# Two half feed-forward units for batches 0 to 3 in place of one full unit

## Chip, cores and metric

The kernel runs on one NeuronCore of a Trainium2 chip. The metric is the device time of one execution in microseconds, of which the median of several runs is taken. The engines are named as in the profile: PE (matrix multiply; PEld is its weight load), DVE (vector), ACT (scalar), POOL (GpSimd) and SP, whose queue issues most transfers.

## What is computed

Top-k attention for 8 batches, 8 heads, 576 tokens and head size 64, followed by a feed-forward block on its 4608 x 512 output:

```python
scores = scale * np.matmul(q, k.transpose(0, 1, 3, 2))
kth = np.partition(scores, -top_k, axis=-1)[..., -top_k:-top_k + 1]
mask = scores >= kth
...
attn = np.exp(scores)
attn = attn / (np.sum(attn, axis=-1, keepdims=True) + 1e-09)
return np.matmul(attn, v).astype(np.float32)
...
h = x @ w_in
g = h - np.tanh(h)
return (g @ w_out).astype(np.float32)
```

Here top_k is 32, w_in is 512 x 2048 and w_out is 2048 x 512. All data are float32.

## The kernel before

**Steps.** The attention is cut into 144 steps, 18 a batch. A main step handles 128 queries of one pair of heads. Since 576 is 4 x 128 + 64, the last 64 tokens of a batch are left over; two remainder steps a batch handle them, each for two pairs of heads. A step's scores are made by PE (L351), copied by ACT (L359) and searched by DVE (L381 to L404) for the 32nd largest value. L381 is the first instruction of a step on DVE. The bank of the scores is read by DVE until L389, and the next step's scores go into the same bank. Then ACT and POOL mask (L437, L440), ACT takes the exponential (L460) and divides (L486), and DVE turns the result in blocks of 32 (L518) into the buffer zx. SP writes zx to DRAM (L531) and reads it back in another order (L534), and five steps later PE multiplies by the values (L582). In batch 0 the turning goes by PE instead. The rows of q and k of batches 1 and 2 are transposed by PE (L311), those of the others by DVE (L318).

**Units.** The attention output, transposed (xT for main tokens, xTr for the leftover ones), goes to the feed-forward block in units. A unit of two blocks has 256 tokens; one of a single block has 128. The leftover 64 tokens of four batches make one unit of 256: batches 0 to 3 and batches 4 to 7. xTr has one buffer.

**Work items.** When a unit's last values are there, `ffn` appends its work to a queue, as items that issue 8 matmuls each (16 records in the profile, since each float32 matmul is recorded twice).
- A full unit has 16 items of `ffn_h` (x @ w_in, tanh, difference): each matmul is split by `by_columns` in two halves of 64 columns of weights with 256 moving columns (L626). Every second item ends with tanh (L652), a copy (L653) on ACT and a difference on POOL (L654). Then come 14 items of `ffn_p`: seven products instead of eight, by a scheme of sums and differences of the quarters. It has the sums made on POOL (L828), its partial results copied by ACT (L909 to L926) and joined on POOL (L877), and two of its right sides, T4 and T2, brought from DRAM by SP (L834).
- A single-block unit has 8 items of `ffn_h` with the full 128 columns of weights and 128 moving columns (L640), and 8 items of `ffn_small_o` (L661). Before the change these are two units of batch 0 only.

When the first full units run, POOL overwrites the upper right corner of each w_out piece by its difference to the upper left one (`combine`, T1), so the products use T1 in place of that corner.

**Order.** Nothing schedules the program afterwards: `run` writes the order by hand. In each step `rate` sets how many items are to be dealt: the smallest rate at which the queue would be empty just when one of the coming units is ready, and at least the one at which a unit's buffer is free in time. `deal` then issues 0.4 of them ahead of the next step's scores, and the rest in three parts of 0.2 behind them. Each engine runs in this order; items that stand ahead of scores on PE come first.

```python
for t, k in coming + [(NS + LAG, 0)]:
    r = have / max(t - n, 1)
    high = r if high is None else min(high, r)
    have += k
...
def deal(part):
    nonlocal credit
    credit += part * share
    while work and credit > 0 and work[0][0] <= usable:
        work.pop(0)[2]()
        credit -= 1
    credit = min(credit, 1.0)
```

Behind the last step a tail remains, in which the last two units run with almost only PE busy. A second pass with an exact search stands behind a branch that is taken only when the fast search failed.

Of the kernel before, what the change touches and what calls it, by code (L numbers as in the profile page):

```python
# [9 lines left out]
ALU = mybir.AluOpType  # L10
FP32 = mybir.dt.float32
# [8 lines left out]
J = 4  # L20
# [35 lines left out]
def kernel(  # L56
# [9 lines left out]
    nc = tc.nc  # L66
    P = nc.NUM_PARTITIONS
    B, H, S, D = q.shape
    DM, DFF = moe_w_in.shape
    NHP = H // 2  # L70
    JP = J * P
    R = S - JP
# [4 lines left out]
    CD = DM // P  # L77
# [5 lines left out]
    WJ = 4  # L83
    FJ = CF // WJ
# [6 lines left out]
    def pool(name, bufs, **kw):  # L91
        return ctx.enter_context(tc.tile_pool(name=name, bufs=bufs, **kw))
# [10 lines left out]
    thpool = pool("th", 4)  # L103
# [7 lines left out]
    bank = [0]  # L111

    def h_bank(k, name):
        return h_ps.tile([P, 512], FP32, tag=f"h{k}", name=name)

    def next_h(name):
        bank[0] ^= 1
        return h_bank(bank[0], name)
# [6 lines left out]
    w_out = [consts.tile([P, FJ, DM], FP32, name=f"w_out{j}") for j in range(WJ)]  # L125
# [91 lines left out]
    def half(t):  # L217
        return slice(t * D, (t + 1) * D)
# [118 lines left out]
    rest = consts.tile([P, 2, S4 + Q], FP32, name="rest")  # L337
# [230 lines left out]
    def values(n):  # L568
# [41 lines left out]
        if n in done:  # L610
            work.extend(ffn(u))
# [9 lines left out]
    cur = {}  # L621

    def by_columns(acc, lhs, rhs, start, stop):

        for t in range(2):
            nc.tensor.matmul(  # L626
                acc[half(t)], lhs[:, half(t)], rhs, start=start, stop=stop, skip_group_check=True
            )
# [45 lines left out]

    def corners(x):
        x = x.rearrange("p (m r) n -> p m r n", r=2)
        return [[x[:, :, r, c * 2 * P : (c + 1) * 2 * P] for c in range(2)] for r in range(2)]

    def keep_corner(j):

        nc.sync.dma_start(kept_B12[:, 2 * j : 2 * j + 2, :], corners(w_out[j][:])[0][1])

    def bring_corners():

        for j in range(WJ):
            nc.sync.dma_start(corners(w_out[j][:])[0][1], kept_B12[:, 2 * j : 2 * j + 2, :])

    def combine(x, j):  # L690

        (b11, b12), (b21, b22) = corners(w_out[j][:])
        k, ms = j // 2, slice(2 * (j % 2), 2 * (j % 2) + 2)
        t2 = whole["T2"][k][:, ms, :]
        if x == "T3":
            nc.gpsimd.tensor_tensor(whole["T3"][k][:, ms, :], b12, b22, ALU.subtract)
        elif x == "T1":
            nc.gpsimd.tensor_tensor(b12, b12, b11, ALU.subtract)
        elif x == "T2":
            nc.gpsimd.tensor_tensor(t2, b22, b12, ALU.subtract)  # L700
            if k == 0:
                outgoing.append((called[0], lambda: nc.sync.dma_start(kept["T2"][:, ms, :], t2)))
        else:
            t4 = temps[j % 2] if k else whole["T4"][k][:, ms, :]
            nc.gpsimd.tensor_tensor(t4, b21, t2, ALU.subtract)
            if k:
                outgoing.append((called[0], lambda: nc.sync.dma_start(kept["T4"][:, ms, :], t4)))
# [242 lines left out]
    def ffn_small_o(u, part):  # L950

        ffn_o(u, 0, part)
        if u.combines:
            combine_next()
# [10 lines left out]
    def ffn(u):  # L965

        nh = CF * u.n // (2 * P)
        full = len(u.blocks) == 2
        if u.tail:
            nh = 0  # L970
            for item in range(2 * len(ORDER)):
                yield CD * WJ, u, lambda item=item: ffn_s(u, item)
        for item in range(nh):
            f = (item + 1) * CF // nh - 1
            yield CD * (f // FJ + 1), u, lambda item=item: (ffn_full if full else ffn_h)(u, item)
        if not full:
            for part in range(CF // 2):
                yield CD * (WJ + part // 2 + 1), None, lambda part=part: ffn_small_o(u, part)
            return
        for item in range(2 * len(ORDER)):  # L980
            yield 2 * WJ * CD, None, lambda item=item: ffn_p(u, item)
# [3 lines left out]
    steps, done, work = [], {}, []  # L985

    def plan():
        steps.clear(), done.clear()

        def block(b, qt):  # L990
            return [(slice(0, P), out[b * S + qt * P : b * S + (qt + 1) * P, :])]

        rest = None
        for b in range(B):
            if b % 4 == 0:
                rest = Unit(
                    [
                        [(half(i), out[(b + k + i) * S + JP : (b + k + i + 1) * S, :]) for i in range(2)]
                        for k in (0, 2)
                    ],  # L1000
                    "xTr",
                )

            parts = [(0, 1), (2, 3)]
            if b == 0:
                parts[0:1] = [(0,), (1,)]
            for a, qts in enumerate(parts):
                unit = Unit([block(b, qt) for qt in qts], "xT")
                unit.tail = b == B - 1 and a == len(parts) - 1
                if unit.tail:  # L1010
                    rest.tail = True
                    unit.items = rest.items = 4 * len(ORDER)
                pe = b == 0
                unit.combines = pe and a == 1
                for hp in range(NHP):
                    for i, qt in enumerate(qts):
                        steps.append(Step(b, hp, qt, unit, 0, i, len(qts), pe, a))
                    if hp == NHP - 1:
                        done[len(steps) - 1] = unit
                    if hp % 2 and a == (0 if b == B - 1 else len(parts) - 1):  # L1020
                        steps.append(Step(b, hp - 1, J, rest, b % 4 * R, pe=pe, part=a))
                        if hp == NHP - 1 and b % 4 == 3:
                            done[len(steps) - 1] = rest
        for g, after in zip(steps, steps[1:]):
            if after.pe and not after.rem and not g.pe:
                g.lag = 3
# [3 lines left out]

    def run(exact):
        plan()
        turned_pe[0] = not exact
        combined[0] = 0
# [237 lines left out]
```

## Time and profile before

| | us |
|---|---|
| median of three runs | 1476.77 |
| lowest, highest | 1475.81, 1477.08 |
| the profiled execution | 1476.01 |
| its span | 1474.2 |
| POOL L440, mask, 288 of 1.435 | 406.8 busy |
| PE L626 hps, 3584 records | 412.2 busy |
| ACT L460, exponential, 288 of 0.776 | 221.9 busy |
| DVE L518, turning, 126 of 1.363 | 171.7 busy |
| POOL L654, difference, 128 of 1.281 | 163.9 busy |
| POOL L828, 128 x 512 sums, 45 of 1.288 (the largest of its groups) | 58.0 busy |
| first and last copy of scores (L359) begin | 10.0, 1333.5 |

The span is what the profiler saw; the execution's own time is 1.8 us longer. "Busy" is the union of a group's instructions. In the waits view a line reads: the engine and line that waited, what released it, then the total in us, how often, and the longest. In the windows view each line is a stretch with its length and each engine's busy time in it; the last three numbers are the granted clock of PE, the busy share of the DMA engines and GB/s. Matmuls are pipelined and their ends modelled, so PE's busy time is an upper reading.

### The profile page before, as it was taken

The numbers are of one execution on the slowest core, as the hardware profiler recorded it, in microseconds if no ns is written. First come the engines' busy times: TensorE is split into PE (matmuls) and PEld (weight loads), VectorE is DVE, ScalarE is ACT, GpSimd is POOL, SyncE is SP. The second block draws the span as 40 slices with busy tenths as digits, with TensorE's granted clock in tenths as the row PEclk, the third lists the DMA queues.
The fourth block names the chain that finished last, engine by engine and source line by source line (L and its number), as shares of the span: only waits on it lengthen the run. The fifth ranks groups of instructions, "written<-read, shape, count | busy, mean of one in ns | idle before, by whom it ended". The sixth has DMA issues, their size and how long they took to land.

```text
span 1474.2 us, 37773 instructions
## 1 busy us (share of the span) xinstructions
PE 1365.6 (93%) x13316; PEld 871.1 (59%) x13316; DVE 1321.5 (90%) x4968; ACT 1033.2 (70%) x1921; POOL 1090.2 (74%) x1581
## 2 busy tenths in 40 slices
PE   4667899889999898999999999999999999999998
PEld 2455565455565555656556666666565666656885
DVE  7999988899999999999999999999999999886411
ACT  4776677778787777777687777777777777664421
POOL 3777679968788686969696969696969697868211
PEclk9787999999999999999999999999999999999999
DMA  9955103676767676686767767777676667643320
GB/s 273 381 184 168 53 21 90 169 195 167 196 173 197 164 183 180 160 209 152 190 152 192 179 174 177 194 168 185 167 184 172 171 167 200 157 141 108 89 53 32
DMA packets 241255, 241.90 MB, mean 164 GB/s; under 512 B 177440, under 2 KB 186144, under 8 KB 233888
## 3 DMA queue, kind: packets, MB, share of 16 engines
q1 hardware_dynamic: 238688, 239.09, 60.7%
q8 instruction: 108, 1.77, 0.5%
q14 instruction: 91, 0.75, 0.2%
q10 hardware_dynamic: 2368, 0.30, 0.2%
HBM read 153.47 MB, written 85.85 MB: 162 GB/s over the span
## 4 chain that ended last, share of the span: by engine, by line
PE 46%; DVE 36%; POOL 9%; DMA 3%; ACT 3%; issue 2%; SPq 0%; DVEq 0%; ACTq 0%; POOLq 0%
PE hps L626 14%; PE hx L626 10%; PE hy L626 8%; DVE m L401 7%; PE av L582 5%; PE scps L351 5%; DVE top L393 5%; DVE rest L404 5%; DVE zx L518 5%; DVE ab L387 3%; POOL z L440 3%; DVE top L404 2%; DVE ab L382 2%; POOL g L654 2%; DVE scps L381 2%
## 5 line engine op out<-in xcount | busy, mean ns | idle before, releaser
L440 POOL TENSOR_TENSOR z<-sc,z 128x576 f32<-128x576 f32 x288 | 406.8, 1435 | 66.4 <-ACT z L437 66.0
L626 PE MATMUL hps<-xT,w_in 128*64 128x256 f32 x3584 | 412.2, 385 | 3.7 <-ACT g L653 3.7
L626 PEld LDWEIGHTS hps<-xT,w_in 128*64 128x64 f32 x3584 | 252.5, 138 | 157.1 <-issue 30.6
L486 ACT ACTIVATE z<-z,rd 128x576 f32<-128x576 f32 x252 | 181.2, 767 | 88.3 <-DVE rd L479 87.9
L460 ACT ACTIVATE z<-z,nb 128x576 f32<-128x576 f32 x288 | 221.9, 776 | 13.1 <-POOL z L440 13.0
L437 ACT ACTIVATE z<-sc,tb 128x576 f32<-128x576 f32 x288 | 208.3, 776 | 24.6 <-POOL tb L418 19.8
L654 POOL TENSOR_TENSOR g<-g,th 128x512 f32<-128x512 f32 x128 | 163.9, 1281 | 63.4 <-ACT g L653 61.9
L393 DVE MAX8 top<-ab 128x8 f32<-128x144 f32 x864 | 194.7, 296 | 0.0
L359 ACT COPY sc<-scps 128x1152 f32<-128x1152 f32 x144 | 161.0, 1118 | 44.7 <-PE scps L351 43.9
L351 PE MATMUL scps<-kT,qT 64*64 64x288 f32 x2016 | 154.6, 422 | 30.3 <-DVE top L389 27.1
L518 DVE STREAM_TRANSPOSE zx<-z 128x1152 f32<-128x1152 f32 x126 | 171.7, 1363 | 7.6 <-ACT z L486 5.1
L401 DVE MAX8 m<-rest 128x8 f32<-128x168 f32 x576 | 161.8, 323 | 0.0
L401 DVE MAX8 m<-top 128x8 f32<-128x144 f32 (+1 forms) x576 | 153.1, 308 | 0.0
L626 PE MATMUL hx<-w_out,g 128*64 128x256 f32 x1088 | 129.2, 385 | 2.5 <-POOL g L654 2.4
L626 PE MATMUL hy<-more,g 128*64 128x256 f32 x1088 | 125.4, 380 | 0.0
L351 PEld LDWEIGHTS scps<-kT,qT 64*64 64x64 f32 x2016 | 66.7, 133 | 97.6 <-issue 26.4
L418 POOL TENSOR_SCALAR tb<-m 128x1 f32<-128x1 f32 x288 | 85.9, 307 | 35.0 <-DVE m L401 34.6
L387 DVE TENSOR_TENSOR ab<-scps,sc 128x576 f32<-128x576 f32 x144 | 107.7, 748 | 0.0
L626 PEld LDWEIGHTS hx<-w_out,g 128*64 128x64 f32 x1088 | 76.2, 138 | 49.9 <-POOL g L654 5.7
L626 PEld LDWEIGHTS hy<-more,g 128*64 128x64 f32 x1088 | 76.7, 137 | 43.7 <-issue 6.7
L652 ACT ACTIVATE th<-hps 128x512 f32<-128x512 f32 x128 | 75.1, 587 | 38.7 <-PE hps L626 35.3
L444 POOL TENSOR_SCALAR bad<-top,tb 128x3 uint8<-128x3 f32 x288 | 96.6, 343 | 0.1
(215 smaller groups left out, 2464.7 us busy)
## 6 DMA issues: line engine op xcount, KB each, us to landing
there<-zx SPq DMA_DIRECT2D x56, 1152.0 KB, 4.8
spare<-there SPq DMA_DIRECT2D x224, 288.0 KB, 5.5
more<-kept_T SPq DMA_DIRECT2D x33, 512.0 KB, 4.2
there<-zx SPq DMA_DIRECT2D x14, 576.0 KB, 7.2
spare<-there SPq DMA_DIRECT2D x56, 144.0 KB, 3.2
out_dram<-ot SPq DMA_DIRECT2D x31, 256.0 KB, 3.0
vb<-in_v_dram SPq DMA_DIRECT2D x48, 128.0 KB, 5.0
kin<-in_k_dram SPq DMA_DIRECT2D x82, 72.0 KB, 4.4
```

The source lines that it names most:

```text
L351: nc.tensor.matmul(ps[i * R : i * R + w, t, s, 0:S2], qT[g.b, hp, g.part][half(t), o : o + w], kT[g.b, hp][half(t), ks], start=True, stop= ...
L359: nc.scalar.copy(sc[:], ps[:, :, :, 0:S2])
L387: nc.vector.tensor_tensor(low[:, :, :, 0:W2], thirds(near), thirds(far), ALU.min)
L393: nc.vector.max(top[:, t, o : o + 8], low[:, t, i, :])
L401: nc.vector.max(m[:, t, m8], seen[i][t])
L437: nc.scalar.activation(zv[:, t, :], scf[:, t, :], AF.Relu, bias=tb[:, t : t + 1], scale=-BIG)
L440: nc.gpsimd.tensor_tensor(zv[:, t, :], scf[:, t, :], zv[:, t, :], ALU.subtract)
L460: nc.scalar.activation(x["zv"][:, t, :], x["zv"][:, t, :], AF.Exp, bias=x["nb"][:, t : t + 1], scale=scale, accum_out=den[:, t : t + 1],)
L486: nc.scalar.activation(x, x, AF.Copy, scale=rds[n][:, g.i, t : t + 1])
L518: nc.vector.transpose(tiles(zx, g.nq)[:, :, :, g.i, :].rearrange("p c k j -> p k c j"), z[:].rearrange("p (k c j) -> p k c j", c=NG, j=G),)
L626: nc.tensor.matmul(acc[half(t)], lhs[:, half(t)], rhs, start=start, stop=stop, skip_group_check=True)
L654: nc.gpsimd.tensor_tensor(g, g, th[:], ALU.subtract)
```

## The change

The leftover tokens of batches 0 and 1 make a single-block unit of 128 tokens, and so do those of batches 2 and 3. Batches 4 to 7 stay one unit of 256. A unit of 128 leftover tokens runs 8 items of `ffn_h` in the wide form (L640), and then 8 items of a new function `ffn_r` in place of products or `ffn_small_o`: four groups of two items, a direct product with w_out in which the upper right corner is T1. The group of the lower left corner adds to the accumulated first group, and the last result gets the first group added by one join on POOL. The T4 and T2 transfers and the sums of `ffn_p` are not needed in such a unit.

```diff
+    def ffn_r(u, item):
+
+        turn, side = item // 2, item // 2 % 2
+        r, c = turn // 2, side
+        if item == 0:
+            cur[u] = [next_h("hx"), None]
+            u.o = thpool.tile([P, DM], FP32, tag="th", name="ot")[:]
+        if item == 2:
+            cur[u][1] = h_bank(bank[0] ^ 1, "hy")
+        acc = cur[u][side][:, 0 : 2 * P]
+        for m in range(4):
+            f = 2 * (4 * (item % 2) + m) + r
+            by_columns(
+                acc,
+                u.g[0][:, f // 4, f % 4 * P : (f % 4 + 1) * P],
+                w_out[f // FJ][:, f % FJ, c * 2 * P : (c + 1) * 2 * P],
+                item in (0, 2) and m == 0,
+                item in (5, 7) and m == 3,
+            )
+        lo, hi = slice(0, 2 * P), slice(2 * P, 4 * P)
+        if item == 1:
+            nc.scalar.copy(u.o[:, hi], acc)
+        elif item == 5:
+            nc.scalar.copy(u.o[:, lo], acc)
+        elif item == 7:
+            y = thpool.tile([P, DM], FP32, tag="th", name="oy")[:]
+            nc.scalar.copy(y[:, hi], acc)
+            nc.gpsimd.tensor_tensor(u.o[:, hi], u.o[:, hi], y[:, hi], ALU.add)
+            for rows, dst in u.blocks[0]:
+                nc.sync.dma_start(dst, u.o[rows, :])
+            bank[0] ^= 1
...
+        if not full and u.tag == "xTr":
+            for item in range(8):
+                yield 2 * WJ * CD, None, lambda item=item: ffn_r(u, item)
+            return
...
+        starts = {0: 2, 2: 4} | {x: x + 4 for x in range(4, B, 4)}
         for b in range(B):
-            if b % 4 == 0:
+            if b in starts:
+                first_b, ends = b, starts[b]
                 rest = Unit(
                     [
-                        [(half(i), out[(b + k + i) * S + JP : (b + k + i + 1) * S, :]) for i in range(2)]
-                        for k in (0, 2)
+                        [(half(i), out[(k + i) * S + JP : (k + i + 1) * S, :]) for i in range(2)]
+                        for k in range(b, ends, 2)
                     ],
                     "xTr",
                 )
...
-                        steps.append(Step(b, hp - 1, J, rest, b % 4 * R, pe=pe, part=a))
-                        if hp == NHP - 1 and b % 4 == 3:
+                        steps.append(Step(b, hp - 1, J, rest, (b - first_b) * R, pe=pe, part=a))
+                        if hp == NHP - 1 and b == ends - 1:
                             done[len(steps) - 1] = rest
```

## The prediction, made before the changed kernel ran

> **What bounds the kernel now.** I read the page's busy shares first, then the clock row, then the windows view by batch, the waits of DVE, and the timeline around one dip of the clock. All times are of the profiled execution (its span is 1474.2 us).
>
> ```profile
> PE 1365.6 (93%) x13316; PEld 871.1 (59%) x13316; DVE 1321.5 (90%) x4968; ACT 1033.2 (70%) x1921; POOL 1090.2 (74%) x1581
> ...
> PEclk9787999999999999999999999999999999999999
> ```
>
> Two engines are nearly full, so which one binds must be asked stage by stage. A step starts with its L381 on DVE. From those starts batch 2 is 371.9 to 527.9 us, batch 3 ends at 685.3, batch 4 at 846.1, batch 5 at 1009.7, batch 6 at 1169.1. In the windows view the columns after the stretch are its length, then PE, PEld, DVE, ACT and POOL busy:
>
> ```profile
> 371.90:527.90 156.00, 151.25 (x1482) 90.90 (x1480) 153.83 (x604) 123.06 (x232) 122.79 (x189) 0.98 0.72 185
> 527.90:685.30 157.40, 147.24 (x1460) 89.43 (x1458) 156.78 (x607) 118.39 (x217) 123.09 (x182) 0.98 0.71 179
> 685.30:846.10 160.80, 157.25 (x1584) 97.02 (x1582) 157.28 (x607) 121.47 (x225) 130.26 (x193) 1.00 0.69 175
> 846.10:1009.70 163.60, 162.98 (x1642) 101.44 (x1640) 157.51 (x607) 122.76 (x228) 129.57 (x194) 1.00 0.70 178
> 1009.70:1169.10 159.40, 156.49 (x1582) 97.14 (x1580) 157.10 (x607) 121.01 (x225) 126.44 (x186) 1.00 0.71 181
> ```
>
> DVE does the same 157 us in each of batches 3 to 6, yet batch 4 takes 160.8 and batch 5 163.6, with PE busy throughout. In batch 3 PE has 10 us to spare. The same view for L626 alone counts the feed-forward matmuls (16 records are one work item):
>
> ```profile
> 371.90:527.90 156.00, 108.89 (x932) 64.95 (x930) 0.98 0.72 185
> 527.90:685.30 157.40, 106.66 (x932) 65.24 (x930) 0.98 0.71 179
> 685.30:846.10 160.80, 118.42 (x1056) 73.52 (x1054) 1.00 0.69 175
> 846.10:1009.70 163.60, 124.28 (x1114) 78.02 (x1112) 1.00 0.70 178
> ```
>
> So batches 2 and 3 carry 58 items each, batch 4 carries 66 and batch 5 69.6. What DVE waits for in batches 2 and 3, and then in 4 and 5:
>
> ```profile
> DVE scps L381 <- ACT sc L359: 1.5, 1, 1.5
> ```
>
> ```profile
> DVE scps L381 <- ACT sc L359: 6.4, 8, 1.2
> DVE zx L518 <- DMA there<-zx: 1.9, 2, 1.6
> ```
>
> The first wait is for the next step's scores, which stand behind feed-forward matmuls in PE's queue. The chain of waits of batch 5 agrees: L626 of hps, hx and hy makes 57% of it, while in batches 2 and 3 DVE lines lead. DVE sets the pace until batch 3, PE does in batches 4 and 5.
>
> The one wait of batches 2 and 3 ends at 500.8 us and has another cause:
>
> ```profile
> 484.72 2.20 PE L351 MATMUL scps<-kT,qT 64*64 64x288 f32 x16 [4.75 <-DVE top L389]
> 486.85 3.68 PE L626 MATMUL hps<-xT,w_in 128*64 128x256 f32 x16
> ```
>
> At step 48 the queue of work is empty; PE idles 4.75 us, and one item then takes 3.68 us because the granted clock is halved from 483.9 to 490.7.
>
> **What the Trainium skill says.** "TensorE: Matmul & The Clock Gate", Part 1, says that an idle window of about 3.4 us halves PE's clock; the trace agrees (4.75 us idle, then an item at twice its price). Its Part 2 says that matmuls stay in program order and only weight loads are pulled ahead: the scores' wait above is what that does. Its LDWEIGHTS section gives columns / 1.2 ns, 107 ns for 128; the trace records 206 ns for such a load, but the pitch of such pairs is 112 ns. "Perfetto Trace Analysis", Identifying the Most-Contended Engine, says that matmul occupancy is a poor measure; it is so here (PE shows 151 of 156 us in batch 2, where DVE leads), so I count work instead.
>
> **Prices.** An item of L626: five run from 1229.41 to 1238.20 us, 1.758 us each. An item at L640 (128 wide weights, 128 columns): eight of ten runs have a pitch of 112 ns, 16 records are 1.79 us; of the two-item runs one took 3.58 and one 3.67 us to the next operation. The row:
>
> ```profile
> L640 PE MATMUL hps<-xT,w_in 128*128 128x128 f32 x256 | 32.4, 287 | 0.0
> ```
>
> Its busy time is 127 ns a record, since it includes half-clock runs. I take 1.80 us, bounds 1.75 (no dearer than the narrow form) and 2.03 (32.4/16). Scores: 1.13 us a step (1238.20 to 1239.33), 20.3 a batch. Values, L582: 21.3 us a batch by the windows view. PE's fixed load is thus 41.6 us a batch. Check: batch 5, 41.6 + 69.6 x 1.758 = 164.0, measured 163.6. Under DVE's 157.3 us there is room for (157.3 - 41.6)/1.758 = 65.8 items. In batch 2, DVE has 153.8 us, and PE's row transposes cost about 2.6 (0.44 us for four, 0.25 for two): room for 62.3.
>
> **The change part by part.**
>
> 1. *Work.* The old four-batch unit has 16 + 14 = 30 items. Each new unit has 8 + 8, so 32 in all: 2 x 1.758 = 3.5 us more, and 16 wide items at +0.04, 0.7 us more: 4.2 us more of PE. Its place decides what that costs.
>
> 2. *Place.* The queue's own arithmetic (rate and deal), carried out for both versions, deals by batch: before 57, 59, 67, 69, 66 in batches 2 to 6; after 62, 62, 65, 65, 66. (PE works through them with some lag, hence 58, 58, 66 and 69.6 above.) It is equal up to step 38. Batches 4 and 5: before 136 items need 239.1 + 83.2 = 322.3 us against DVE's 314.8, over by 7.5; the measured waits are 8.3. After, 130 items need 228.5 + 0.3 (eight wide ones) + 83.2 = 312.0, under by 2.8. The wait for scores should go, but for unevenness: I leave 2.0 us, of which the transfer of zx may be most. Gain 6.3 us; bounds 3 (half of it comes back) and 8.3 (all of it).
>
> 3. *Batch 2.* It gets 62 items with 62.3 of room, unevenly: steps 39 to 47 get 32 instead of 30. They need 32 x 1.758 + 9 x 1.13 + 4 x 2.2 + 1.8 (remainder values) + 1.4 (transposes) = 78.4 us against 76.5. Carrying PE's lag from step to step, with a lag of about 3.5 us free (a step of 8.47, less 2.6 until L389 frees the scores' bank, 1.13 for scores, 1.2 for L359), leaves 2.4 us of wait, at steps 40 and 46. Bounds 0 and 5 (an item at 1.81). Step 48's two items let it catch up. Batch 3: 62 against 65.8, nothing.
>
> 4. *Clock.* Steps 48, 57 and 66, which got 0, 1 and 0 items, get 2, 2 and 1. The idle stretch at 480 goes, and with it the wait of 1.5 us. Bounds: 1.5 gain, 0 if the dip comes anyway.
>
> 5. *Batches 6 and 7.* The same counts, but at step 111 one item fewer waits and a few steps get 5 and 4 in another order. The same step-by-step carrying gives 1.0 us more. Bounds -2 and +3. The tail after step 143 is unchanged.
>
> 6. *POOL, ACT.* Per unit of products gone: six sums of 1.28 us, four of 0.735 (L828), three joins of 0.74 (L877); two joins come. POOL is 11.4 us lighter; ACT loses seven copies of 0.365 and gets six. Worth nothing of itself: the windows show POOL busy for 79 to 81% of batches 4 and 5, and DVE waits for it nowhere there. If its cover goes, PE's waits for L828 (2.4 us in batches 4 and 5) shrink, inside item 2's bounds. ffn_r's second item waits for the last L654 as the products' second did, once more than before: 0 to 1.3 us (the longest wait of hx for POOL in this stretch), hidden in PE's free lag. The copy of acc at item 1 has two items (3.5 us) before item 4 writes there.
>
> 7. *SP and buffers.* Two transfers of 512 KB (T4, T2) go; no wait names them. The four output transfers stay, in two pairs, and stand ahead of the next L531 on SP's queue; the second pair needs a join on POOL first. The 1.6 us wait of L518 at 871 us followed such a pair (issue 866.75, the zx transfer 867.97). Cost 0 to 1.6 each; I take 0, since only one output of batches 4 and 5 was followed by such a wait. The xTr buffer (one) is read out at steps 47 to 49 and 86 to 88, before the next remainder values at 53 and 89.
>
> Sum: -6.3 + 2.4 - 1.5 + 1.0 = -4.4 us. The profiled execution itself took 1476.0 us, 0.8 below the median of 1476.8; so 1471.6 there, 1472.4 for the median.
>
> **The rivals.**
>
> *Eaten by batch 2 (1476.5 us).* Two items and 4.2 us more of PE, with batch 2 at 62 of 62.3: the wait there becomes 5 instead of 2.4 and the clock dips all the same (0 instead of -1.5), while batches 4 and 5 give 6.3 and batches 6 and 7 take 1: sum -0.3. For it: PE shows no idle time between 397 and 474 us already. Against: the item's price held for all of batch 5. This also covers a gain that only moves into batches 6 and 7.
>
> *Wide weights (1480 us, slower).* In ffn_h a half unit loads 128 columns for only 128 moving ones. If these loads are not hidden, at steps 47 to 49 and 86 to 88, each of the 256 records costs its load, up to 206 ns instead of 112: 24 us. At 150 ns it adds 9.7 us, of which about 2 find room: -4.4 + 7.7 = +3.3. It decides from a pitch of 112 + 4400/256 = 129 ns. For it: 206 ns loads, one run at 151 ns. Against: eight of ten runs at 112, the others where the clock was halved.
>
> **How the numbers follow.** Forecast 0.55, eaten 0.26, slower 0.19. The forecast's own range: 1467.5 to 1474.5 (bounds of items 2 to 5, not all at once). A measurement of this kernel can tell about 0.2%, 3.0 us: below 1473.8 is faster, above 1479.7 slower. Of the forecast nine tenths are faster, 0.50; with a part of the second case, 0.56. Same takes the rest of both and a third of the slower case's near end: 0.29. Slower: 0.15. Range 1467.5 to 1479.5: it leaves out the slower case's upper part and a little below.
>
> **What would show it.** Right: batches 4 and 5 at about 158 us each, the wait of L381 there below 2.5 us, no half clock near 480 us, L640 of xTr at 112 ns, batch 2 with 2 to 3 us of waits. Wrong: L381 waiting 5 us in batch 2, L518 waiting for zx after the new output pairs, or waits past 1010 us that grow by more than 3 us.

## The result, and the profile after

The changed kernel takes 1468.8 us (median, 1467.3 to 1470.1), the kernel before, measured beside it, 1475.7 us. The ratio is 0.9953, 95% interval 0.994 to 0.9966: 6.9 us less, between 5.0 and 8.9. The profiled execution took 1468.75 us with a span of 1467.0, against 1476.01 and 1474.2: 7.2 us less span. The forecast was 4.4 us less.

The windows view of the changed kernel, batches 2 to 6 by the starts of L381 (length, then PE, PEld, DVE, ACT, POOL busy):

```profile
370.60:528.90 158.30, 157.03 (x1560) 101.19 (x1560) 154.31 (x604) 121.81 (x232) 118.71 (x184) 1.00 0.70 182
528.90:686.30 157.40, 151.42 (x1526) 93.67 (x1524) 156.78 (x608) 119.50 (x222) 125.83 (x188) 1.00 0.71 179
686.30:847.50 161.20, 155.90 (x1560) 101.79 (x1558) 157.14 (x607) 120.00 (x222) 125.57 (x187) 1.00 0.69 175
847.50:1008.40 160.90, 156.76 (x1584) 97.36 (x1582) 157.18 (x607) 120.54 (x225) 125.47 (x188) 1.00 0.68 173
1008.40:1167.00 158.60, 154.66 (x1564) 95.95 (x1562) 157.24 (x607) 120.98 (x223) 127.08 (x185) 1.00 0.71 181
```

DVE's work is the same as before to 0.5 us in every batch, so each difference of length is a wait. Batch 2 grew by 2.2 us, batch 3 kept its 157.4, batch 4 grew by 0.4, and batch 5 lost 2.7. PE is no longer busy through the whole of batch 5 (156.8 of 160.9 us; before 163.0 of 163.6). Taken to the end, the starts of L381 give this account of the 7.2 us:

| stretch | before, us | after, us | difference | forecast |
|---|---|---|---|---|
| batch 0 | 199.9 | 198.7 | -1.2 | 0 |
| batch 1 | 160.9 | 160.9 | 0.0 | 0 |
| batch 2 | 156.0 | 158.3 | +2.2 | +0.9 |
| batch 3 | 157.4 | 157.4 | 0.0 | 0 |
| batches 4 and 5 | 324.4 | 322.1 | -2.3 | -6.3 |
| batches 6 and 7 | 324.9 | 319.4 | -5.5 | +1.0 |
| after the last L381 | 139.5 | 139.1 | -0.4 | 0 |

(Batch 7 is counted to its last L381.) Batch 0 runs the same order in both; a second profile of the changed kernel took 201.2 us for it, so its 1.2 us are chance. Batches 2 to 5, where the work was moved, give 0.1 us together (1.1 in a second pair of profiles). The largest gain stands where none was forecast.

DVE's waits of the changed kernel in batches 2 and 3:

```profile
DVE scps L381 <- ACT sc L359: 2.9, 4, 1.4
DVE zx L518 <- ACT z L486: 0.4, 1, 0.4
```

and in batches 4 and 5:

```profile
DVE zx L518 <- DMA there<-zx: 5.5, 5, 2.5
DVE scps L381 <- ACT sc L359: 1.0, 2, 0.6
```

The wait for scores fell from 6.4 to 1.0 us, as forecast. But the wait for the zx transfer rose from 1.9 to 5.5 us: before L518 may overwrite zx, the last transfer from it must have landed.

In batch 7 the kernel before has one wait that the changed kernel lacks. Its line in the waits view (1305 to 1320 us of the kernel before):

```profile
DVE scps L381 <- ACT sc L359: 3.6, 1, 3.6
```

and PE's timeline there, start, length and what:

```profile
1304.70 6.17 PE L626 MATMUL hps<-xT,w_in 128*64 128x256 f32 x54
1313.20 3.62 PE L626 MATMUL hps<-xT,w_in 128*64 128x256 f32 x16 [2.33 <-ACT g L653]
1316.75 1.20 PE L351 MATMUL scps<-kT,qT 64*64 64x288 f32 x16
```

The scores stand behind six items (96 records, of which the view shows the last 70). The sixth waits 2.33 us for ACT to empty its bank, and then takes 3.62 us instead of 1.76, because the granted clock was halved from 1313.3 to 1316.7 us. In the changed kernel the scores of the same step follow six items too, but without a gap:

```profile
1299.20 10.75 PE L626 MATMUL hps<-xT,w_in 128*64 128x256 f32 x96
1309.88 1.20 PE L351 MATMUL scps<-kT,qT 64*64 64x288 f32 x16
```

So PE has the same work ahead of these scores. What differs is ACT's order. In the kernel before, the tanh and the copy that empty the bank (L652, L653) stand behind the mask and the division of the step (L437, L486), and L486 waits for DVE:

```profile
1307.02 1.47 ACT L437 ACTIVATE z<-sc,tb 128x576 f32<-128x576 f32 x2
1310.75 1.44 ACT L486 ACTIVATE z<-z,rd 128x576 f32<-128x576 f32 x2 [2.27 <-DVE rd L479]
1312.10 0.57 ACT L652 ACTIVATE th<-hps 128x512 f32<-128x512 f32 x1
1312.58 0.57 ACT L653 COPY g<-hps 128x512 f32<-128x512 f32 x1
```

In the changed kernel they stand ahead of both:

```profile
1304.65 0.60 ACT L652 ACTIVATE th<-hps 128x512 f32<-128x512 f32 x1 [0.15 <-PE hps L626]
1305.14 0.58 ACT L653 COPY g<-hps 128x512 f32<-128x512 f32 x1
1305.60 1.45 ACT L437 ACTIVATE z<-sc,tb 128x576 f32<-128x576 f32 x2
1308.11 1.44 ACT L486 ACTIVATE z<-z,rd 128x576 f32<-128x576 f32 x2 [1.05 <-DVE rd L479]
```

### The profile page after: what moved, and what is told of

Same layout as the page of the kernel before. It is cut to its first block, busy times and chain, and to the rows that moved or that the text cites. A ratio compares the mean times of both kernels' runs of the same rounds, so it can differ in the third digit from the quotient of the medians.

```text
span 1467.0 us, 37814 instructions
## 1 busy us (share of the span) xinstructions
PE 1362.4 (93%) x13348; PEld 884.6 (60%) x13348; DVE 1321.2 (90%) x4968; ACT 1028.8 (70%) x1920; POOL 1078.9 (74%) x1570
## 4 chain that ended last, share of the span: by engine, by line
PE 40%; DVE 39%; DMA 8%; POOL 7%; ACT 3%; issue 2%; SPq 1%; DVEq 0%; ACTq 0%; POOLq 0%
PE hps L626 12%; PE hx L626 9%; DVE m L401 7%; PE hy L626 7%; DVE zx L518 5%; DVE top L393 5%; DVE rest L404 5%; PE av L582 5%; PE scps L351 4%; DMA there<-zx 3%; DVE ab L387 3%; POOL z L440 2%; DVE top L404 2%; DVE ab L382 2%; DVE scps L381 2%
## 5 line engine op out<-in xcount | busy, mean ns | idle before, releaser
L626 PE MATMUL hps<-xT,w_in 128*64 128x256 f32 x3584 | 405.6, 381 | 0.6 <-ACT g L653 0.6
L486 ACT ACTIVATE z<-z,rd 128x576 f32<-128x576 f32 x252 | 181.2, 767 | 123.7 <-DVE rd L479 121.2
L437 ACT ACTIVATE z<-sc,tb 128x576 f32<-128x576 f32 x288 | 208.4, 777 | 19.3 <-POOL tb L418 14.4
L654 POOL TENSOR_TENSOR g<-g,th 128x512 f32<-128x512 f32 x128 | 163.9, 1281 | 63.5 <-ACT g L653 62.4
L518 DVE STREAM_TRANSPOSE zx<-z 128x1152 f32<-128x1152 f32 x126 | 171.4, 1360 | 10.6 <-DMA there<-zx 6.2
L626 PE MATMUL hx<-w_out,g 128*64 128x256 f32 x1152 | 137.2, 386 | 10.5 <-POOL g L654 8.7
L626 PE MATMUL hy<-more,g 128*64 128x256 f32 x1024 | 119.2, 381 | 0.2 <-ACT ot L944 0.2
L626 PEld LDWEIGHTS hx<-w_out,g 128*64 128x64 f32 x1152 | 82.4, 139 | 59.6 <-POOL g L654 12.7
L626 PEld LDWEIGHTS hy<-more,g 128*64 128x64 f32 x1024 | 71.9, 137 | 42.2 <-issue 5.9
L652 ACT ACTIVATE th<-hps 128x512 f32<-128x512 f32 x128 | 75.0, 586 | 30.4 <-PE hps L626 22.6
```

What stands on the lines that cost most here:

```text
L437: nc.scalar.activation(zv[:, t, :], scf[:, t, :], AF.Relu, bias=tb[:, t : t + 1], scale=-BIG)
L486: nc.scalar.activation(x, x, AF.Copy, scale=rds[n][:, g.i, t : t + 1])
L518: nc.vector.transpose(tiles(zx, g.nq)[:, :, :, g.i, :].rearrange("p c k j -> p k c j"), z[:].rearrange("p (k c j) -> p k c j", c=NG, j=G),)
L626: nc.tensor.matmul(acc[half(t)], lhs[:, half(t)], rhs, start=start, stop=stop, skip_group_check=True)
L654: nc.gpsimd.tensor_tensor(g, g, th[:], ALU.subtract)
```

## The experiments

The median of the kernel before, measured beside each group of runs, is given with each; it moved between 1475.5 and 1476.0 us. Theory: the leftover work's place gains in batches 4 and 5 and costs in batch 2, and batch 7's gain is a rounding of the dealing. Rivals: the form of the half units gains, or the moved work reaches batch 7, or the waits wander by chance.

### Batch 7: the rounding of one item

By the queue's arithmetic the kernel before enters step 140 with 0.13 less credit than the changed kernel. It deals 3 items there and 8 in step 141, four of these ahead of the scores; the changed kernel deals 4 and 7, three ahead. So one item, and with it the emptying of its bank on ACT, passes from step 140 to the head of step 141; the six items between the scores stay six. First, the kernel before with that credit:

```diff
             share, usable, now[0] = rate(), converted[0], n
+            if n == 140:
+                credit += 0.13
```

> The kernel before, with 0.13 added to the dealing credit at step 140, so that the fourth item falls into step 140 instead of the head of step 141 (the only difference in the order dealt). Theory: the 3.65 us wait of DVE at 1315 us, which the changed kernel does not have, comes from this rounding alone, and 3 to 4.5 us of the change's gain with it: about 1472 us where the kernel before has 1476. Rival: the wait came from the half clock at 1313 us by chance, or from work that the change moved: then within 1 us of the kernel before.

Measured: 1471.4 us against 1476.0; ratio 0.9962 (0.9947 to 0.9977). Batch 7 took 161.3 us to its last L381 instead of 165.6, and no DVE wait stands between 1300 and 1318 us. The counts of items between scores are as in the kernel before (96 and 112 records), and the gap of 2.33 us on PE is gone. Nothing else was changed, so up to 4.3 us of the change's gain hang on one item's place.

The same the other way round, 0.13 taken from the changed kernel at step 140:

```diff
             share, usable, now[0] = rate(), converted[0], n
+            if n == 140:
+                credit -= 0.13
```

> The changed kernel, with 0.13 taken from the credit at step 140, so that steps 140 and 141 get 3 and 8 items as in the kernel before. Theory (rounding): 3 to 4.5 us slower than the changed kernel, about 1472 us instead of 1468.8, with a wait of over 3 us before L381 near 1308 us. Rival (the gain in batch 7 is the moved work's): within 1 us of the changed kernel.

Measured: 1471.7 us, ratio 0.9972 (0.996 to 0.9984), 2.9 us over the changed kernel's median, which was not measured beside it; batch 7 took 163.4 us instead of 160.8. The wait came back, but shorter than expected. Its line:

```profile
DVE scps L381 <- ACT sc L359: 2.0, 1, 2.0
```

Here the clock was full throughout (1.00 between 1305 and 1317 us; 0.86 in the kernel before). So 2.0 us of the 3.6 are the item's place, and the other 1.6 the half clock on top of it.

The half clock does not follow from the order alone. Within each of the 14 profiles, from batch 1 on, all half-clock stretches begin a whole number of 3.413 us apart (in the kernel before 483.87 and 1313.31 us: 243 of them), as if the clock were set window by window. By PE's recorded matmuls, PE was idle for more than 2.05 us of such a window 55 times in all profiles between batch 1 and the last scores, and a half clock followed every time; below 1.90 us none began. The gap of 2.33 us lies whole in one window in both profiles of the kernel before (1309.90 to 1313.31 us in the first). Four other kernels here have the same gap, the late version below among them; there a window's edge cuts it, no half clock follows, and the wait is 2.0 us each time.

### Form without place

Both half units as in the change, but given to the queue only at step 76, when the full unit was ready before:

```diff
+        if u.xT is None and u.pair is not None:
+            u.xT = xt(u.pair)
...
-                    u.xT[:, c, 0:w],
+                    u.xT[:, c, u.off : u.off + w],
...
-            work.extend(ffn(u))
+            for x in held.pop(u, []) + [u]:
+                work.extend(ffn(x))
...
+            if n == 138:
+                credit = -0.82
```

> The two half units as in the change, but both given to the queue at step 76, where the four-batch unit was ready before (they share its xTr buffer, 128 columns each); the credit at step 138 is set to the value of the kernel before. Form without place: 137 items in batches 4 and 5 instead of 136 before and 130 after. Theory (place is what gains): 2 to 5 us slower than the kernel before, 1478 to 1481 us, with waits of L381 of 8 to 12 us in batches 4 and 5. Rival (the form gains: no products, fewer sums on POOL, no T4 and T2 transfers): faster than the kernel before by 2 us or more, near 1472 us.

Measured: 1481.2 us against 1476.0, ratio 1.0034 (1.0022 to 1.0045). Batch 4 took 169.8 us and batch 5 160.4, together 5.8 us more than before. The waits there (L381 is line 382 in this kernel):

```profile
DVE scps L382 <- ACT sc L360: 12.5, 10, 3.4
DVE zx L519 <- ACT z L487: 1.1, 2, 0.9
```

The form alone loses; the lighter POOL and the two transfers fewer earn nothing that shows. The loss is near the 4.2 us of extra PE work that the prediction counted. (Batch 7, without the half clock, is 2.1 us shorter in this profile than in that of the kernel before, so the two profiles differ by 4.1 us.) Against the changed kernel with the same rounding (1471.7), place alone is worth 9.5 us.

### The idle stretch at step 48

The kernel before, with its 30 items of steps 39 to 47 spread over steps 39 to 48, so that PE has work in step 48:

```diff
             share, usable, now[0] = rate(), converted[0], n
+            if 39 <= n <= 48:
+                share = 3.05
+            if n == 138:
+                credit = -0.82
```

> The kernel before with the rate set to 3.05 items in steps 39 to 48, so that step 48 gets 3 items instead of none; the credit at step 138 is pinned. Theory (the wait of 1.5 us at 499 us comes from PE's idle stretch and the half clock after it): no half clock between 470 and 500 us and no wait there, 1.5 us faster, 1474.5 us. Rival (the wait comes from the values and scores alone): the wait stays, and the time.

Measured: 1472.7 us against 1475.5, ratio 0.9982 (0.9972 to 0.9993). The windows view from 470 to 500 us of the kernel before, and then of this one:

```profile
470.00:500.00 30.00, 25.25 (x216) 13.78 (x210) 29.23 (x116) 20.63 (x39) 17.85 (x32) 0.89 0.63 175
```

```profile
470.00:500.00 30.00, 28.67 (x278) 17.18 (x279) 29.90 (x127) 22.43 (x41) 19.13 (x31) 1.00 0.77 206
```

The clock stays at 1.00 instead of 0.89, and DVE's wait of 1.5 us is gone. So the wait comes from how these steps are dealt. The edit takes the idle stretch and the half clock away together, so how much of the 1.5 us each causes is not shown. Batch 2 is 1.3 us shorter in this profile. Batch 7 is 2.1 us shorter, since its wait is 2.0 us instead of 3.6, with no half clock there; whether that makes up the rest of the median's gain is not shown.

### Both repairs, and no half units

> The kernel before with both repairs of its dealing: 3.05 items in steps 39 to 48, and the credit of step 140 raised by 0.13. Theory (both are separate from the place of the leftover work): the waits of 1.5 and 3.7 us go, 1470.5 us, against the changed kernel's 1468.8, so that the moved work itself is worth about 2 us once L518's new waits are paid. Rival (the repairs overlap or bring other waits): 1473 us or more.

```diff
             share, usable, now[0] = rate(), converted[0], n
+            if 39 <= n <= 48:
+                share = 3.05
+            if n == 138:
+                credit = -0.82
+            if n == 140:
+                credit += 0.13
```

Measured: 1468.6 us against 1475.5, ratio 0.9946 (0.993 to 0.9961). The changed kernel, run again beside it, took 1468.9 us (0.9949, 0.9934 to 0.9965). The expected 1470.5 was too slow: two repairs of the dealing alone reach what the change reaches, within the intervals. Batches 4 and 5 still wait as before (5.8 us for scores, 1.7 for zx), and batch 2 takes 154.3 us where the changed kernel takes 158.3.

### Do the waits repeat?

> The kernel before once more, for a second profile. Theory: of the 3.65 us wait at 1315 us, 2.0 are the rounding of the credit (in every run) and the rest a half clock near 1313 us that falls there by chance: the wait is 2.0 or 3.7 us, the waits of batches 4 and 5 (6.4 us of L381) stand at the same places. Rival: the waits wander as a whole, and no sum by place can be trusted.

> The changed kernel once more, for a second profile beside the other runs of this call: 1468 to 1470 us, L381 waiting about 3 us in batch 2 and 1 us in batches 4 and 5, L518 waiting 4 to 6 us there if its place in the order causes it; below 2 us if it was chance.

The kernel before took 1475.9 us and showed the same waits to 0.3 us: 1.5 at 500 us, those of batches 4 and 5 at the same places, and 3.6 at 1316 us, with the clock halved there again. The changed kernel waited 2.3 us for scores at steps 40 to 46 and 1.0 in batches 4 and 5, and 4.6 us for zx there. The waits are the order's, not chance, but for the 1.6 us of the half clock in batch 7: the two profiles of the kernel before have the 3.413 us windows at the same place to 0.03 us, and whether that is chance is not shown.

### The new waits for zx

In the changed kernel the zx transfer (L531) goes out 2.0 us after the end of L518 at 999 us, and 2.2 and 2.4 us after it at 820 and 858 us; usually it takes 0.03 us. At 999 us SP stands at the T2 transfer ahead of it (L866 in the changed kernel), whose buffer PE must first have read. SP's waits from 990 to 1000 us:

```profile
SPq L866 <- PE hy L626: 8.0, 1, 8.0
SPq L531 <- DVE ab L388: 0.2, 1, 0.2
```

The two other late ones stand behind output transfers. At 820 us it is the pair of a full unit (L961) and the four L534 behind it:

```profile
814.77 3.48 SPq L961 DMA_DIRECT2D out_dram<-ot  x2
818.36 1.81 SPq L534 DMA_DIRECT2D spare<-there  x4
820.27 0.38 SPq L531 DMA_DIRECT2D there<-zx  x1
```

At 858 us it is the new pair of a half unit, which stood from 849.6 to 857.2 us; no wait of DVE over 0.6 us came of that one.

A transfer can also land late. A zx transfer of a main step (1152 KB) lands 4.8 us after its issue in the median; behind T2 it took 7.0 us at 810 and 6.9 at 999 us, where the kernel before has 4.7 and 4.4. The smaller one of a remainder step (576 KB) takes 7.0 us in the median; the one at 820 us is of this kind.

So T2 was issued two items later:

```diff
-        if item == 11 and not (u.tail and u.tag == "xT"):
+        if item == 13 and not (u.tail and u.tag == "xT"):
             bring("T2")
```

> The changed kernel, with the transfer of T2 issued in the last item of a unit (item 13) instead of item 11, so that SP does not stand waiting for the matmul that last reads the buffer (8.2 and 8.0 us waits of that transfer just ahead of the two zx transfers at 809 and 999 us). Theory (the new waits of L518, 5.5 us in batches 4 and 5, come from SP's queue, where the T2 transfer stands ahead of the zx transfer): these waits fall to 2 us or less, 1465 to 1467 us. Rival (they come from the other transfers' load or from values that are late on PE): within 1 us of the changed kernel, L518's waits as before.

Measured: 1466.1 us against 1475.5, ratio 0.9931 (0.9918 to 0.9944, which just meets the changed kernel's interval). Batches 4 and 5 took 319.0 us instead of 322.1, with these waits:

```profile
DVE zx L518 <- DMA there<-zx: 2.8, 3, 1.9
DVE scps L381 <- ACT sc L359: 1.0, 2, 0.6
```

The waits at 729 and 1005 us are gone, and the transfers at 810 and 997 us land after 4.7 and 4.5 us. So T2 cost twice at 999 us: it held SP's queue, and the transfer behind it landed later. One wait of 1.9 us at 826 us stayed, more than expected. There the zx transfer goes out in time behind four L534 transfers, at 818.8 us, and lands some 8.6 us later. It is the 576 KB transfer of a remainder step; the kernel before has it at 818.7 us with 7.2 us, and nothing waits for it there. So not every wait for zx is SP's queue, and what slows these landings was not tried.

The same line in the kernel before:

> The kernel before, with the T2 transfer issued in item 13 instead of item 11. Theory: L518 waits only 1.9 us in batches 4 and 5 there, so at most 1 to 2 us are to be had: 1474 to 1476 us. Rival (the T2 transfer delays the zx transfer of many steps without a wait that shows): 3 us or more faster.

Measured: 1476.0 us against 1475.5, ratio 1.0003 (0.9992 to 1.0014). One wait for zx, at 871 us, grew from 1.7 to 3.2 us, and a new one of 1.6 us came at 1239 (the changed kernel with this edit has one of 2.2 us at the same step). The edit helped only where the T2 transfer happened to stand ahead of a zx transfer.

### Evening out batch 2

The changed kernel with its rate capped:

```diff
             share, usable, now[0] = rate(), converted[0], n
+            if 39 <= n <= 50:
+                share = min(share, 3.35)
+            if n == 138:
+                credit = -0.69
```

> The changed kernel with the rate of dealing capped at 3.35 items a step in steps 39 to 50, what PE has room for there; the credit at step 138 is set to the changed kernel's. Batches 2 to 6 get 60, 62, 66, 66, 66 items. Theory: the 3.1 us of waits at steps 40 to 46 go and little comes back, since batch 3 has room: 1466 us, 2.5 us below the changed kernel. Rival: the two more items in batches 4 and 5 bring 2 to 3 us of waits back there: no difference within 1 us.

Measured: 1471.7 us against 1476.0, ratio 0.9959 (0.9943 to 0.9974); the expectation failed. Batch 2 did fall from 158.3 to 155.5 us. But batch 3 took 1.5 us more (a wait for zx), batch 4 1.0 more and batch 6 3.3 more, with a half clock at 1052 us ahead of its first wait. The likely reason, which was not tested apart, is that every later item stands elsewhere in its step. The waits of its batches 4 and 5:

```profile
DVE zx L518 <- DMA there<-zx: 4.2, 2, 2.2
DVE scps L381 <- ACT sc L359: 2.8, 2, 2.4
```

With both edits, the cap and the later T2:

> The changed kernel with both the cap of 3.35 items in steps 39 to 50 and the T2 transfer in item 13. If the cap's gain of 2.8 us in batch 2 was eaten by L518 waiting for zx at 664, 825 and 1003 us (5.7 us in all), these fall below 2 us and the time is 1466 to 1468 us; if it was eaten by the scores' waits of batches 4 and 6 (5.5 us), about 1471 us.

Measured: 1468.7 us against 1475.5, ratio 0.9947 (0.9934 to 0.996). The zx wait at 1003 us went, those at 668 and 829 us stayed (1.1 and 2.4 us), and so did the scores' waits of batches 4 and 6 (in a profile of the slowest of five executions, 1473.2 us): between the two outcomes that were expected.

### A faster version

The later T2 with a milder cap:

```diff
             share, usable, now[0] = rate(), converted[0], n
+            if 39 <= n <= 46:
+                share = min(share, 3.5)
+            if n == 138:
+                credit = -0.69
...
-        if item == 11 and not (u.tail and u.tag == "xT"):
+        if item == 13 and not (u.tail and u.tag == "xT"):
```

> The changed kernel with the T2 transfer in item 13 and a milder cap, 3.5 items a step in steps 39 to 46 (62, 62, 65, 66, 66 items in batches 2 to 6 by the queue's arithmetic, give or take one). If the waits in batch 2 are those of the crowded dealing and the cap leaves the order in batches 4 to 6 nearly as it was, the time is 1464 to 1465 us, 1 to 2 us below the kernel with the T2 transfer moved alone; if every shift of the order brings waits back elsewhere, as the harder cap did, 1467 us or more.

Measured: 1465.0 us against 1476.0, ratio 0.9928 (0.9913 to 0.9943): 11 us below the kernel before, and 3.8 us below the changed kernel, which was not measured beside it and whose interval (0.994 to 0.9966) just meets this one. Batch 2 took 156.0 us and batches 4 and 5 319.8. Its lead of 1.1 us over the kernel with the later T2 alone lies within the intervals.

## Why the prediction was right, and where it was not

The direction and the range held; 1472.4 was forecast and 1468.8 came. That the total came so near is luck: batches 2 to 5, on which the forecast of -5.4 us rested, gave -0.1, and batches 6 and 7, forecast at +1.0, gave -5.5.

1. *Work.* Right in size. Two items and 16 wide ones more, and the late version lost 5.2 us where PE has no room, for a counted 4.2. A wide item cost 1.835 us (four of them from 815.82 to 823.16), not 1.80: 0.6 us over both units. The rival of wide weights falls: 64 records in 7.34 us are a pitch of 115 ns, and it decided from 129.

2. *Place, batches 4 and 5.* The mechanism was right, a term of the sum was mis-sized. The waits for scores fell by 5.4 us, to 1.0. But "I leave 2.0 us, of which the transfer of zx may be most" was too little: the zx waits alone are 5.5 us, 4.6 in the second profile. The net gain was 2.3 us instead of 6.3, below the lower bound of 3. The prediction counted two transfers fewer as "no wait names them" and the rest of SP's queue at nothing. It did not ask where the remaining T2 and output transfers would come to stand when every item moves in its step. Moving T2 gave 3.1 us of it back (2.3 against the second profile). What it named as a sign of being wrong, a new output pair ahead of zx, made one transfer 2.4 us late without a long wait.

3. *Batch 2.* Right: 2.4 us of waits at steps 40 and 46 were forecast, 2.9 came, at steps 40, 42 and 46. The batch itself grew by 2.2 us instead of 0.9, since DVE also had 0.5 us more work and a wait of 0.4 us for ACT. The rival in which this eats the gain had the wrong size here (its 5 us did not come), but its -1.3 us for batches 2 to 5 is nearer to the measured -0.1 than the forecast's -5.4.

4. *Clock.* Right, -1.5 us: no half clock stands near 480 us after the change, and filling step 48 in the kernel before removes the same wait. Far less idle time than the 4.75 us there is enough for a half clock: 2.33 us were, in batch 7.

5. *Batches 6 and 7.* Wrong, and the largest term: +1.0 was forecast, -5.5 came. The step that failed is "The same counts, but ... a few steps get 5 and 4 in another order". It carried PE's items from step to step, and these are indeed the same: six items stand ahead of the scores in both kernels. It names no term there for an item that waits until ACT has emptied its bank, and that is the 2.33 us which went. Nor was the kernel before's own wait at 1316 us, the second longest for scores, looked into.

6. *POOL, ACT.* Right as far as shown: POOL's busy time fell by 11.3 us (forecast 11.4; 9.1 in the second pair of profiles), and the late version, which has the same lighter POOL, was slower. The second item of `ffn_r` waited up to 1.94 us for L654 (at 840 us), over the bound of 1.3, but no wait of DVE for scores followed.

Set against the kernel before with both repairs (1468.6), the moved work itself nets nothing that shows: batches 4 and 5 are 1.3 us shorter, with more waits for zx, and batch 2 is 4.0 us longer. It seems to pay once those waits are mended, 1466.1 and 1465.0 us; the interval of the latter (0.9913 to 0.9943) still overlaps that of the repaired kernel (0.993 to 0.9961), so how much is not settled. Whether a repaired kernel before could be brought lower by other dealing was not tried.

## What to carry to other kernels

Where two engines are both nearly full and the order is written out by hand, cost a change by stretches as room on one engine against work on the other. Then carry the order itself through to the end, on every engine that an item needs: a shift of an eighth of an item put one emptying of a bank behind other work on ACT some nine hundred microseconds later, and moved 2.6 to 4.3 us, with the same items ahead of the same scores on PE. Before crediting a gain to a change, repair the same stretch in the old kernel by a line that has nothing to do with the change. Count also what stands ahead of each transfer in its queue, not only the transfers added or removed.

## What was not expected of the hardware

A transfer that waits for its buffer held the transfers behind it in SP's queue: the T2 transfer stood 8.0 us, and the zx transfer behind it went 2.0 us late. It also landed 6.9 us after its issue, against 4.4 us for that step's transfer in the kernel before.

The larger zx transfer is the faster one: 1152 KB land in 4.8 us (median of 56 in each profile), 576 KB in 7.0 to 7.2 (median of 14). Why was not tried.

The half clock comes in windows of 3.413 us at fixed distances. In these profiles more than 2.05 us without a matmul inside one window was always enough to begin it, and less than 1.90 us never; in between it went both ways. So the same gap of 2.33 us cost a wait of 3.6 us in two profiles and of 2.0 us in four others.
